# A top-32 attention and squared-ReLU feed-forward kernel: w_in in eight loads, a longer early form, fetches behind the transposes, later reciprocals and another order in the tail

## The chip, the cores and the metric

The kernel runs on one core of one Trainium2 chip. The metric is the device time of one execution in microseconds, the median of three timed runs. A separate profiled execution gives the rows shown here; times inside it count from the start of its span.

## The reference

```python
def _attn_ref(q, k, v):                      # q, k, v: (8, 8, 576, 64) float32
    scores = (1.0 / np.sqrt(64)) * np.matmul(q, k.transpose(0, 1, 3, 2))
    kth = np.partition(scores, -32, axis=-1)[..., -32:-31]
    scores = np.where(scores >= kth, scores, -1000000000.0)
    scores = scores - np.max(scores, axis=-1, keepdims=True)
    attn = np.exp(scores)
    attn = attn / (np.sum(attn, axis=-1, keepdims=True) + 1e-09)
    return np.matmul(attn, v)

def _moe_ref(x, w_in, w_out):                # (4608, 512), (512, 2048), (2048, 512)
    h = np.maximum(x @ w_in, 0.0)
    return h * h @ w_out
# reference: x is the attention output with its heads side by side, one row a token
```

Each of 64 heads has 576 queries. A query keeps its 32 highest scores, takes the softmax over them and weighs the values. The result goes through a feed-forward layer with a squared ReLU.

## The kernel before

**Steps.** Heads are taken in 32 pairs, four to a batch. One pair has 576 rows of scores for each of its two heads, cut into chunks of 128 rows. A step of the main loop handles two such chunks (the two heads of a pair, or the 64-row rests of two pairs), and there are U = 144 steps. Steps 0 to 3 belong to pair 0, step 4 to the rests of pairs 0 and 1, steps 5 to 8 to pair 1; from step 9 on pairs 2 and 3 alternate. The program is one order written out by hand: `pin` keeps every instruction in program order on its engine, so an instruction that waits holds back all that stands behind it on the same engine.

**What a step does.** In step u the VectorE (DVE) first combines scores into candidates (`quads_of`, lines 323 and 324) and then runs four rounds of `topk`: eight maxima by MAX8 (line 374), and their removal by MATCH_REPLACE8 (line 378) after each round but the last. TensorE (PE) computes the scores of step u+1 into the banks `sc_a` and `sc_b` (line 285), and ScalarE (ACT) copies both into `s` (line 294). Between rounds 2 and 3 the DVE begins step u+1 with `pairs_of` (lines 314, 315 and, in the early form, 317). GpSimd (POOL) computes the lesser candidates (`both`, line 338, and `lesser`, line 347), which round 3 of the step reads, and marks the dropped scores (`drop`, line 411). ACT takes exponentials of step u-3 (`exps`, line 423) into `w_two`, `turn` has the SP queue transpose them by DMA into `wT` (line 432), and PE multiplies with the values two steps later (`weigh`, line 467; `in_gap` puts this between the two halves of the scores). `invert` takes the reciprocal of the sums on the DVE (line 483, or line 487 for the last 24 steps, where the sums come out of PE), and `place` scales the result into `x_tok` on ACT (line 506) or, where asked, on the DVE (line 504).

**The early form.** For u < EARLY the DVE computes the minimum of one quarter itself (line 317), and POOL's two lesser operations are half as wide (288 elements instead of 576). For u < EARLY - 2, `drop` adds its marks to `s` on POOL (line 413); after that an accumulating DMA from the POOL queue does it (line 415).

**Loading the heads.** `load_pair(i)` puts the ten loads of a pair on a list, `fetch(n)` issues the next n of them on the SP queue. The raw tiles have two buffers each. `prepare(u)` runs the next of the four units of a pair: the PE transposes and ACT copies of q and of k (`main`, lines 174 and 175), the 64-row rests (`rest`), and the copy of the values. A pair may be begun from `due(i) - 4` on: steps 1, 3 and 5 for pairs 1, 2 and 3. The transposes of a pair stand in PE's order behind the scores of the next step.

**Loading the weights.** `w_loads` holds four loads of `w_in` (128 rows of 2048 each, read as two groups of 64 rows in DRAM) and four of `w_out`. They go on POOL's queue and convert from float32 to bfloat16. `load_weights(1)` stands before the first scores, behind the first `lesser`, and at the end of each step, so `w_in` is issued by the end of step 1 and `w_out` in steps 2 to 5.

**The feed-forward and the tail.** Whenever 128 rows of `x_tok` are full, PE transposes them, multiplies with `w_in`, ACT takes ReLU and square, and PE multiplies with `w_out`; pieces of this are spread over the steps. Behind the loop the last two steps are masked on the DVE (line 427), transposed by PE (line 449), copied (`turned`, lines 454 and 456), weighed, placed, and the last 128 rows go through the feed-forward layer; `halves` (line 627) is the last product.

Of the kernel before, what the change touches and what calls it, by code (L numbers as in the profile page):

```python
# [23 lines left out]
def kernel(  # L24
# [41 lines left out]
    w_in = const.tile([128, KH, d_ff], bf16, name="w_in")  # L66
# [61 lines left out]
    def fetch(n):  # L128
        while n and fetches:
            fetches.pop(0)[1]()  # L130
            n -= 1
# [130 lines left out]
    U = len(steps)  # L262
    first = {}
# [42 lines left out]
    def pairs_of(u):  # L306
# [8 lines left out]
        pin(tt(near, one[:, :, 0:QUAR], two[:, :, 0:QUAR], op=ALU.max))  # L315
        if u < EARLY:
            pin(tt(cat[:, :, HALF + QUAR:S], one[:, :, QUAR:HALF], two[:, :, QUAR:HALF], op=ALU.min))
# [9 lines left out]
    def copy_far(u):  # L327
        d = st[u]
        if u >= EARLY:
            pin(nc.scalar.activation(d["most"][:, 1], d["ps"][1][:, :, 0:QUAR], AF.Copy))  # L330

    def both(u):
        d = st[u]
        n_h = 1 if u < EARLY else 2
        wide = n_h * QUAR
# [4 lines left out]
    def lesser(u):  # L340
        d = st[u]
        n_h = 1 if u < EARLY else 2
        wide = n_h * QUAR
# [3 lines left out]
        pin(tt(less, less, d["most"][:, 0:n_h, :, :].bitcast(i32).rearrange("p h x n -> p x h n"), op=ALU.subtract))  # L347

    GROUP = 18
    EARLY = 9  # L350
    held_m = {}
    tests = []

# [2 lines left out]
    def topk(u, rounds=(0, 1, 2, 3)):  # L356
        d = st[u]
        g = u % GROUP
        if g == 0 and 0 in rounds:
            held_m["m"] = small.tile([128, GROUP, 2, 4, 8], f32, name="m", bufs=2)  # L360
        held = held_m["m"]
        m = d["m"] = [held[:, g, :, r] for r in range(4)]
        d["ends"] = held[:, g].rearrange("p x r j -> p x (r j)")[:, :, 0:32:31]
        cat = d["cat"]
        def part(r, x):
            if r == 0:
                return cat[:, x, 0:QUAR].rearrange("p (g n) -> p g n", n=18)[:, :, 0:13]
            if r == 1:
                return cat[:, x, 0:QUAR].rearrange("p (g n) -> p g n", n=6)[:, :, 1:6]
            return cat[:, x, 0:(HALF - 24, S)[r - 2]]  # L370

        for r in rounds:
            for x in range(2):
                pin(nc.vector.max(out=m[r][:, x, :], in_=part(r, x)))  # L374
            if r == 3:
                break
            for x in range(2):
                pin(nc.vector.match_replace(out=part(r, x), in_to_replace=m[r][:, x, :], in_values=part(r, x), imm_value=NEG))  # L378
        if g == GROUP - 1 and 3 in rounds:
            f0 = 2 * (u + 1 - GROUP)  # L380
            each = held[:, :, :, :, 7].rearrange("p g x r -> p (g x) r")
            at = flags[:, f0:f0 + 2 * GROUP]
            for r in range(3):
                tests.append(lambda r=r: nc.gpsimd.tensor_tensor(at[:, :, r], each[:, :, 3], each[:, :, r], op=ALU.subtract))
            tests.append(lambda: nc.gpsimd.tensor_mul(at[:, :, 3], each[:, :, 3], each[:, :, 3]))
            tests.append(lambda: nc.gpsimd.tensor_scalar(at[:, :, 3], at[:, :, 3], scalar1=-1.0, scalar2=TINY * TINY, op0=ALU.mult, op1=ALU.add))
# [10 lines left out]
    SUMMED = U - 24  # L397
# [43 lines left out]
    def turn_by_tensor(u, x):  # L441
        if "tp" not in st[u]:
            st[u]["wT"] = scp.tile([128, 9, 128], bf16, name="wT", bufs=4)
            st[u]["tp"] = {}
        flat = w_two[u % 3][:, :, :].rearrange("p x n -> p (x n)")
        tp = bank(2 * (u - U + 2) + x, [128, 1024], bf16)
        tp = st[u]["tp"][x] = tp[:, 0:512 + 128 * x].rearrange("p (n r) -> p n r", r=128)
        for n in range(4 + x):
            pin(nc.tensor.transpose(tp[:, n, :], flat[:, (4 * x + n) * 128:(4 * x + n + 1) * 128], id_h[:, :]))

    def turned(u, x, by_scalar):
        to, tp = st[u]["wT"][:, 4 * x:4 + 5 * x, :], st[u]["tp"][x]
        if by_scalar:
            pin(nc.scalar.activation(to, tp, AF.Copy))
        else:
            pin(nc.vector.tensor_copy(to, tp))
# [22 lines left out]
    def invert(u):  # L479
        if u < SUMMED:  # L480
            if u % 2 == 0:
                both_r = small.tile([128, 2, 2, 1], f32, name="rboth", bufs=4)
                pin(nc.vector.reciprocal(both_r[:, :, :, 0], st[u]["sums"][:, :, :]))
                st[u]["r"], st[u + 1]["r"] = both_r[:, 0], both_r[:, 1]
            return
        r = small.tile([128, 2, 1], f32, name="rsum", bufs=4)
        pin(nc.vector.reciprocal(r[:, :, :], sums(u)[:, :, 64:65]))
        st[u]["r"] = r
# [231 lines left out]
    def to_weigh(u):  # L720
        return u - 5 if u <= CATCH + 1 else u - 4

    def in_gap(u):
        products(to_weigh(u))
        if moves:
            moves.pop(0)()()
# [25 lines left out]

    w_loads = []
    for kh in range(KH):
        rows = moe_w_in.rearrange("(t e a d) n -> t a e d n", t=2, e=2, a=2)[kh // 2, kh % 2]
        w_loads.append((w_in[:, kh, :], rows))
    for g in range(4):
        rows = moe_w_out.rearrange("(f p) n -> p f n", p=128)[:, 4 * g:4 * g + 4, :]
        w_loads.append((w_out[:, 4 * g:4 * g + 4, :], rows))

    def load_weights(n):
        for to, rows in w_loads[:n]:
            pin(nc.gpsimd.dma_start(out=to, in_=rows))
        del w_loads[:n]
# [9 lines left out]
    def due(i):  # L774
        if i >= NP - 8:
            return 101 + 4 * (i - (NP - 8))
        return first[4 * (i // 4) + 3] - 1 - 4 * (3 - i % 4) if i >= 4 else 2 * i + 3

    def prepare(u):
        nonlocal coming  # L780
# [11 lines left out]
    ones = const.tile([128, 1], f32, name="ones")  # L792
    pin(nc.gpsimd.memset(ones[:, :], 1.0))
    worst = const.tile([128, 1], f32, name="worst")
    load_weights(1)
    scores(0)
    both(0)
    copy_far(0)
# [8 lines left out]
    def ok(w):  # L807
        return 0 <= w < U
# [16 lines left out]
    for u in range(U):  # L825
        at_step[0] = u
        for x in range(2):
            if ok(u - 1) and not by_vector(u - 1, x):
                drop(u - 1, x)
        quads_of(u)  # L830
        topk(u, (0,))
        if u == U - 1:
            break
        if ok(u + 1):
            for i, c, a in steps[u + 1]:
                while coming <= i or (coming == i + 1 and soon):
                    prepare(u)
            scores(u + 1, (lambda: in_gap(u)) if u else None)
            both(u + 1)
        if u == 0:  # L840
            in_gap(u)
        if ok(to_weigh(u)):
            invert(to_weigh(u))
        casts_next = bool(soon) and soon[0].__name__ == "values"
        for _ in range(0 if casts_next else 2 if u < 8 else 1):
            prepare(u)
        if ok(to_weigh(u)):
            place(to_weigh(u))
        turn_x(u)
        moves.extend(soon_moves)  # L850
        soon_moves.clear()
        if u < 6:
            fetch(4)
        w = to_raise(u)
        if ok(w):
            exps(w, 0)
            exps(w, 1)
            turn(w)
        if u >= 6:
            fetch(4 if u < 12 else 3)  # L860
        topk(u, (1, 2))
        if u == U - 2:
            while behind:
                behind.pop(0)()
            take("d")
            products(u - 3)
            take("d")
        if ok(u + 1):
            pairs_of(u + 1)
            if u == U - 2:  # L870
                invert(u - 3)
            copy_far(u + 1)
            lesser(u + 1)
            if tests:
                pin(tests.pop(0)())
        if u == U - 2:
            place(u - 3)
            turn_x(u)
            take("d", True)
            moves.pop(0)()()  # L880
        if u == CATCH:
            exps(u - 2, 0)
            exps(u - 2, 1)
            turn(u - 2)
        topk(u, (3,))
        if casts_next:
            prepare(u)
        while after_far:
            after_far.pop(0)()
        after_far.extend(next_far)  # L890
        next_far.clear()
        if u < U - 2:
            dense(u, 0)
        st[u]["neg"] = negate(u, 2)
        if u == CATCH + 1:
            products(u - 4)
            invert(u - 4)
            place(u - 4)
            turn_x(u)
        if u < U - 2:  # L900
            dense(u, 1)
        else:
            early_exps(u, 1)
        load_weights(1)
# [30 lines left out]
    turned(U - 1, 0, False)  # L935
    products(U - 3)
    turn_by_tensor(U - 1, 1)
    turned(U - 1, 1, False)
    products(U - 2)
    products(U - 1)  # L940
    three.relu()
    invert(U - 4)
    invert(U - 3)
    place(U - 4)
    place(U - 3)
    three.square(nc.gpsimd)
# [2 lines left out]
    invert(U - 2)  # L949
    place(U - 2, (True, True))  # L950
    invert(U - 1)
    place(U - 1, (True, False))
    four.relu()
    four.square(nc.gpsimd)
    by_hand.clear()
# [155 lines left out]
```

## Time and profile before

| what | value |
|---|---|
| median of 3 timed runs | 915.57 us (914.55 to 915.66) |
| profiled execution, its own time | 914.72 us |
| span of the profiled execution | 912.6 us |
| mean granted TensorE clock | 0.939 |
| DVE busy | 873.8 us (96% of the span) |
| ACT busy | 779.4 us (85%) |
| POOL busy | 778.2 us (85%) |
| PE busy | 671.4 us (74%) |
| bytes moved by DMA | 165.98 MB, mean 182 GB/s |

Busy time is time in which an engine executes instructions. A row of the timeline gives the start and the duration in us, the engine, the line in the kernel, the operation, output <- inputs, the shape and the number of merged instructions; in square brackets stands how long the engine was idle just before, and what released it. A name like PEq or SPq is an engine's own queue. DMA rows give the size of one transfer and the median time from issue to landing. q0 is the queue that POOL's loads use, q1 that of SP. A queue's share is that of 16 DMA engines over the window.

### The profile page before, as it was taken

Reading aid. Unit: us, or ns where it says so; the run is one execution under the profiler, and the core shown is the slowest. Engines: PE = TensorE matmul, PEld = TensorE weight load, DVE = VectorE, ACT = ScalarE, POOL = GpSimd, SP = SyncE. Lnnn points to the kernel's source line nnn. Section 1 sums busy time; section 2 is a strip of 40 time slices with the busy share of each in tenths; the row PEclk is TensorE's granted clock in tenths of the full one; section 3 lists DMA queues with packets and bytes.
Section 4 is the critical chain, followed back from the end, with each engine's and each line's share of the span. In section 5 each row is a group of like instructions: output and inputs, shape, how many; then the busy total and the mean of one; then the engine's idle time right before and its main releaser. Section 6 shows DMA issues by size and latency. Waiting matters only on the chain.

```text
span 912.6 us, 20980 instructions
## 1 busy us (share of the span) xinstructions
PE 671.4 (74%) x6190; PEld 424.8 (47%) x6268; DVE 873.8 (96%) x3567; ACT 779.4 (85%) x1996; POOL 778.2 (85%) x816
## 2 busy tenths in 40 slices
PE   6276778677777777777776777777677677888886
PEld 3133345444444444544454544544444454555555
DVE  6759999999999999999999999999999999999995
ACT  3256789988998999988999899999999998998994
POOL 7669888988899888998898988998889988898892
PEclk9789999999998999998999999999999999989999
DMA  5778997999898999898889899898989999977972
GB/s 114 138 126 164 185 190 160 205 193 198 190 202 188 197 203 198 194 181 199 196 193 195 173 201 207 196 187 199 219 191 197 189 209 210 161 168 155 180 168 52
DMA packets 294586, 165.98 MB, mean 182 GB/s; under 512 B 261697, under 2 KB 272193, under 8 KB 294465
## 3 DMA queue, kind: packets, MB, share of 16 engines
q1 hardware_dynamic: 267408, 80.29, 46.9%
q0 software_dynamic: 25712, 83.84, 40.5%
q8 instruction: 52, 0.85, 0.4%
q14 instruction: 70, 0.57, 0.2%
q10 hardware_dynamic: 1344, 0.43, 0.2%
HBM read 37.75 MB, written 9.44 MB: 52 GB/s over the span
## 4 chain that ended last, share of the span: by engine, by line
DVE 66%; issue 12%; ACT 10%; PE 5%; SPq 5%; DMA 2%; ACTq 0%
DVE m L374 28%; DVE cat L378 18%; DVE sc_b L314 6%; DVE most L315 5%; DVE cat L324 5%; DVE cat L323 5%; SPq L117 2%; ACT s L294 2%; SPq L110 1%; ACT h L610 1%; DMA q_raw<-in_q_dram 1%; ACT rl L602 1%; PE dn_ps L661 1%; PE sc_b L285 1%; PE gen L595 1%
## 5 line engine op out<-in xcount | busy, mean ns | idle before, releaser
L374 DVE MAX8 m<-cat 128x8 f32<-128x104 f32 (+3 forms) x1152 | 437.5, 420 | 0.0
L378 DVE MATCH_REPLACE8 cat<-m,cat 128x104 f32<-128x104 f32 (+2 forms) x864 | 262.0, 310 | 0.0
L338 POOL TENSOR_TENSOR cat<-s 128x576 int32<-128x576 int32 (+1 forms) x144 | 240.1, 1668 | 3.0 <-ACT s L294 3.0
L347 POOL TENSOR_TENSOR cat<-cat,most 128x576 int32<-128x576 int32 (+1 forms) x144 | 196.9, 1367 | 26.7 <-ACT most L330 12.6
L285 PE MATMUL sc_b<-qkT 64*128 64x288 f32 x512 | 105.8, 488 | 87.6 <-DVE cat L324 83.6
L595 PEld LDWEIGHTS <-w_in 128*128 128x128 bf16 x2304 | 149.0, 102 | 41.5 <-issue 20.3
L285 PE MATMUL sc_a<-qkT 64*128 64x288 f32 x512 | 97.9, 455 | 82.6 <-DVE most L315 61.3
L661 PE MATMUL dn_ps<-w_out,h 128*128 128x512 bf16 x478 | 143.0, 421 | 10.6 <-issue 6.8
L595 PE MATMUL gen<-xT,w_in 128*128 128x128 bf16 x1984 | 137.6, 226 | 3.5 <-ACT xT L550 2.9
L411 POOL TENSOR_SCALAR gone_b<-s,neg 128x576 uint8<-128x576 f32 x142 | 105.9, 746 | 29.1 <-ACT neg L394 17.5
L411 POOL TENSOR_SCALAR gone_a<-s,neg 128x576 uint8<-128x576 f32 x143 | 106.7, 746 | 13.6 <-ACT neg L394 2.0
L294 ACT ACTIVATE s<-sc_b 128x576 f32<-128x576 f32 x144 | 93.2, 647 | 22.2 <-PE sc_b L285 16.3
L294 ACT ACTIVATE s<-sc_a 128x576 f32<-128x576 f32 x144 | 91.2, 633 | 5.5 <-PE sc_a L285 3.7
L285 PEld LDWEIGHTS sc_a<-qkT 64*128 64x128 f32 x512 | 41.7, 188 | 110.6 <-issue 56.0
L285 PEld LDWEIGHTS sc_b<-qkT 64*128 64x128 f32 x512 | 43.4, 196 | 102.8 <-PE av_ps L467 61.5
L610 ACT ACTIVATE h<-rl 128x512 bf16<-128x512 f32 x136 | 85.7, 630 | 4.3
L602 ACT ACTIVATE rl<-gen 128x512 f32<-128x512 f32 x140 | 81.8, 584 | 3.0 <-PE gen L595 2.9
L314 DVE TENSOR_TENSOR sc_b<-sc_a,s 128x288 f32<-128x288 f32 x144 | 65.3, 454 | 18.8 <-ACT s L294 16.3
L661 PEld LDWEIGHTS <-h 128*128 128x128 bf16 x544 | 51.8, 105 | 64.0 <-issue 31.3
L467 PEld LDWEIGHTS <-wT 128*128 128x128 bf16 (+1 forms) x1600 | 54.7, 100 | 56.7 <-issue 45.6
L415 POOL DMA_DIRECT2D s<-gone_b x68 | 60.0, 883 | 22.0 <-DVE m L374 12.0
L394 ACT ACTIVATE neg<-m 128x4 f32<-128x4 f32 (+1 forms) x145 | 29.9, 207 | 57.2 <-DVE m L374 56.3
(186 smaller groups left out, 1296.5 us busy)
## 6 DMA issues: line engine op xcount, KB each, us to landing
s<-gone_b POOLq DMA_DIRECT2D x68, 576.0 KB, 4.6
s<-gone_a POOLq DMA_DIRECT2D x67, 576.0 KB, 4.6
v_raw<-in_v_dram SPq DMA_DIRECT2D x64, 128.0 KB, 3.0
k_raw<-in_k_dram SPq DMA_DIRECT2D x63, 128.0 KB, 3.2
q_raw<-in_q_dram SPq DMA_DIRECT2D x63, 128.0 KB, 3.3
out_dram<-wide SPq DMA_DIRECT2D x31, 256.0 KB, 2.9
v_raw<-in_v_dram SPq DMA_DIRECT2D x64, 32.0 KB, 3.2
w_in<-in_moe_w_in_dram POOLq DMA_DIRECT2D x4, 512.0 KB, 24.6
```

The lines of the kernel that those rows point to most:

```text
L285: pin(nc.tensor.matmul(out=ps[j][:, x, 0:HALF], lhsT=lhsT, rhs=rhs, start=True, stop=True))
L294: pin(nc.scalar.activation(s[:, :, j * HALF:(j + 1) * HALF], ps[j][:, :, 0:HALF], AF.Copy))
L314: pin(tt(far, one[:, :, QUAR:HALF], two[:, :, QUAR:HALF], op=ALU.max))
L338: pin(tt(less, s[:, :, 0:wide].bitcast(i32), s[:, :, HALF:HALF + wide].bitcast(i32), op=ALU.add))
L347: pin(tt(less, less, d["most"][:, 0:n_h, :, :].bitcast(i32).rearrange("p h x n -> p x h n"), op=ALU.subtract))
L374: pin(nc.vector.max(out=m[r][:, x, :], in_=part(r, x)))
L378: pin(nc.vector.match_replace(out=part(r, x), in_to_replace=m[r][:, x, :], in_values=part(r, x), imm_value=NEG))
L411: pin(nc.gpsimd.tensor_scalar(byte[:, x, :, 1], s[:, x, :], scalar1=d["neg"][:, x, 1:2], scalar2=-HUGE, op0=ALU.add, op1=ALU.mult))
L595: pin(nc.tensor.matmul(out=hp[:, n * n_rows:(n + 1) * n_rows], lhsT=w_in[:, kh, (f0 + n) * 128:(f0 + n + 1) * 128], rhs=xt(kh), start=(kh ...
L602: pin(nc.scalar.activation(kept["rl"][:, :], hp, AF.Relu))
L610: pin(nc.scalar.activation(h2, flat, AF.Square))
L661: pin(nc.tensor.matmul(out=op[:, :], lhsT=held["h2"][:, f, c * 128:(c + 1) * 128], rhs=w_out[:, f, :], start=(f == 0), stop=(f == NF - 1)))
```

## The change

Six edits are made at once.

- `w_in` is loaded in eight loads of 64 rows: each half of a former load is a DMA of its own, whose DRAM side is 64 rows and not two groups of 64. Two halves are issued ahead of the first scores, one behind the first `lesser`, one at the end of each of steps 0 to 4; `w_out` follows in steps 5 to 8.
- `EARLY` is 11 and not 9: steps 9 and 10 take the early form, and `drop` of steps 7 and 8 adds on POOL.
- Pairs 1, 2 and 3 may be begun at steps 1, 4 and 7.
- `fetch` stands behind `turn` in the first six steps too, as it did later.
- In the steps with `to_weigh(u) >= SUMMED` and u < U - 5 (125 to 138), round 1 of `topk` goes ahead of the reciprocal and not behind it.
- In the tail the reciprocals of U-4 and U-3 go ahead of the last copy of `turned`, and both results of U-1 are placed by the DVE, where ACT had one.

```diff
-    EARLY = 9
+    EARLY = 11
...
     for kh in range(KH):
-        rows = moe_w_in.rearrange("(t e a d) n -> t a e d n", t=2, e=2, a=2)[kh // 2, kh % 2]
-        w_loads.append((w_in[:, kh, :], rows))
+        for e in range(2):
+            rows = moe_w_in.rearrange("(t e a d) n -> t a e d n", t=2, e=2, a=2)[kh // 2, kh % 2, e]
+            w_loads.append((w_in[64 * e:64 * e + 64, kh, :], rows))
...
-        return first[4 * (i // 4) + 3] - 1 - 4 * (3 - i % 4) if i >= 4 else 2 * i + 3
+        return first[4 * (i // 4) + 3] - 1 - 4 * (3 - i % 4) if i >= 4 else 3 * i + 2
...
-    load_weights(1)
+    load_weights(2)
     scores(0)
     both(0)
     copy_far(0)
...
             in_gap(u)
+        sums_late = ok(to_weigh(u)) and to_weigh(u) >= SUMMED and u < U - 5
+        if sums_late:
+            topk(u, (1,))
         if ok(to_weigh(u)):
             invert(to_weigh(u))
...
-        if u < 6:
-            fetch(4)
         w = to_raise(u)
         if ok(w):
             exps(w, 0)
             exps(w, 1)
             turn(w)
-        if u >= 6:
-            fetch(4 if u < 12 else 3)
-        topk(u, (1, 2))
+        fetch(4 if u < 12 else 3)
+        topk(u, (2,) if sums_late else (1, 2))
...
     products(U - 3)
     turn_by_tensor(U - 1, 1)
+    invert(U - 4)
+    invert(U - 3)
     turned(U - 1, 1, False)
     products(U - 2)
     products(U - 1)
     three.relu()
-    invert(U - 4)
-    invert(U - 3)
     place(U - 4)
     place(U - 3)
...
     invert(U - 1)
-    place(U - 1, (True, False))
+    place(U - 1, (True, True))
```

## The prediction

> **What bounds the kernel now.** I read the busy shares first, then who waited for whom, then the windows, to see where the bounding engine stands still.
>
> ```profile
> PE 671.4 (74%) x6190; PEld 424.8 (47%) x6268; DVE 873.8 (96%) x3567; ACT 779.4 (85%) x1996; POOL 778.2 (85%) x816
> DVE sc_b L314 <- ACT s L294: 16.3, 3, 15.8
> DVE rsum L487 <- PE av_ps L467: 1.4, 2, 0.9
> 40.00:46.00 6.00, 0.00 (x0) 0.00 (x0) 0.14 (x1) 0.00 (x0) 0.00 (x0) 0.50 0.82 146
> 160.00:400.00 240.00, 176.85 (x1670) 114.63 (x1687) 239.75 (x984) 219.85 (x576) 213.80 (x214) 0.94 0.93 195
> ```
>
> The DVE is the bound: from 160 to 400 us it is busy 239.75 of 240 us. Only fewer DVE instructions or fewer DVE waits shorten the kernel. Its waits (columns: total, times, longest) hold one large entry, a single stop of 15.8 us. In the window from 40 to 46 us (columns: length, busy PE, PEld, DVE, ACT, POOL, then clock, DMA share, GB/s) no engine computes while the DMA engines are 82% busy. So the loads ended last there. The timeline of that stretch says which.
>
> ```profile
> 39.73 0.41 DVE L378 MATCH_REPLACE8 cat<-m,cat 128x264 f32<-128x264 f32 x1
> 49.61 1.11 PE L174 MATMUL gen<-id_f,k_raw 128*128 128x128 f32 x4 [13.54 <-DMA q_raw<-in_q_dram]
> 55.94 0.47 DVE L314 TENSOR_TENSOR sc_b<-sc_a,s 128x288 f32<-128x288 f32 x1 [15.80 <-ACT s L294]
> 57.04 1.41 DVE L374 MAX8 m<-cat 128x8 f32<-128x576 f32 x2
> ```
>
> L314 at 55.94 begins step 5, which works on pair 1, whose heads are long there. Ahead of its scores PE has the transposes of pair 2's k, moved forward into step 3, and those wait until 49.61 for the load. Why is a load so late? The DMA view has it, first for 16 to 23 us, then for 24 to 30, then for 78 to 130.
>
> ```profile
> q0 software_dynamic: 756, 0.44, 36.4%
> w_in<-in_moe_w_in_dram POOLq DMA_DIRECT2D x1, 512.0 KB, 23.8
> q0 software_dynamic: 655, 0.56, 51.1%
> k_raw<-in_k_dram SPq DMA_DIRECT2D x2, 128.0 KB, 20.3
> k_raw<-in_k_dram SPq DMA_DIRECT2D x4, 128.0 KB, 3.4
> w_in<-in_moe_w_in_dram POOLq DMA_DIRECT2D x4, 512.0 KB, 24.6
> s<-gone_b POOLq DMA_DIRECT2D x68, 576.0 KB, 4.6
> ```
>
> With three w_in loads in flight, q0 holds 36.4% of 16 engines, 5.8 of them; with four, 51.1%, 8.2. So each w_in load runs on two engines, and takes 24.6 us. The accumulating DMA of the same queue moves more, 576 KB, in 4.6 us. What differs is the source: w_in is read as two groups of 64 rows, the other as 128 rows. A k load of 128 KB landed in 20.3 us while the weights were in flight and in 3.4 us later: every head load waits for its share on the engines that w_in holds.
>
> **The change part by part.**
>
> *EARLY 11: +0.7.* The starts of L314 give the step.
>
> ```profile
> 62.31 0.46 DVE L314 TENSOR_TENSOR sc_b<-sc_a,s 128x288 f32<-128x288 f32 x1
> 68.60 0.46 DVE L314 TENSOR_TENSOR sc_b<-sc_a,s 128x288 f32<-128x288 f32 x1
> 87.25 0.45 DVE L314 TENSOR_TENSOR sc_b<-sc_a,s 128x288 f32<-128x288 f32 x1
> 93.19 0.45 DVE L314 TENSOR_TENSOR sc_b<-sc_a,s 128x288 f32<-128x288 f32 x1
> ```
>
> An early step takes 68.60 - 62.31 = 6.29 us, a later one 93.19 - 87.25 = 5.94. Two steps at 0.35 make +0.7, on the bounding engine, hidden by nothing.
>
> *Halves of w_in, and pair 2 a step later: -15.8.* A half is one group of 64 rows. If the rows are dealt out to 16 engines, each gets 4 instead of 64, and 24.6 us become an estimated 24.6 / 16 = 1.5 us plus the fixed part, bounded by the 4.6 us row above.
>
> The Trainium skill speaks for and against. Its page "DMA: Bandwidth & Descriptors" says under "Rules for kernel authors" that splitting a transfer into two partition halves is not worth it, as both use the same 16 engines; by this the stop would shrink by its later place alone (a rival below). Its section "Why a DMA increments its semaphore by 16 and not by 1" says the slowest dimension of both sides sets the number of engines: two before, sixteen after. The 36.4% and 51.1% bear the second one out; the premise of the first is not met here.
>
> ```profile
> 12.03 1.82 SPq L110 DMA_DIRECT2D q_raw<-in_q_dram  x2
> 13.89 10.85 SPq L117 DMA_DIRECT2D q_raw<-in_q_dram  x1
> 28.79 0.72 PE L285 MATMUL sc_a<-qkT,qbd_a 128*128 128x288 f32 x2 [1.36 <-DVE cat L317]
> ```
>
> Pair 2's loads begin at 12.03 and SP is then held 10.85 us in one issue, as the queue backs up. Unheld, the first eight of its ten loads, at 1.82 / 2 = 0.91 us an issue, are out by 19.3 us and with 3.4 us landed by 23. Their transposes now stand behind the scores of step 5, one step of 6.3 us after those of step 4 at 28.79, so not before 35 us: 12 us to spare. Then L314 of step 5 starts where step 4 ends, 39.73 + 0.41 = 40.14, and the whole 15.8 us go. The next thing due, pair 3, is fetched in steps 4 to 6 and transposed in step 7.
>
> *Four more weight loads on POOL: 0, up to +2.3.* POOL's issues and round 3 of the step are the pair to watch.
>
> ```profile
> 11.50 0.79 POOL L338 TENSOR_TENSOR cat<-s 128x288 int32<-128x288 int32 x1 [1.95 <-ACT s L294]
> 36.42 0.79 POOL L347 TENSOR_TENSOR cat<-cat,most 128x288 int32<-128x288 int32 x1
> 58.94 0.79 POOL L763 DMA_DIRECT2D w_out<-in_moe_w_out_dram  x1
> 65.69 0.79 POOL L763 DMA_DIRECT2D w_out<-in_moe_w_out_dram  x1
> 66.56 0.74 POOL L411 TENSOR_SCALAR gone_b<-s,neg 128x576 uint8<-128x576 f32 x1
> 72.58 0.75 POOL L411 TENSOR_SCALAR gone_a<-s,neg 128x576 uint8<-128x576 f32 x1
> ```
>
> The extra load ahead of the first scores (0.79, as for w_out) fits into the 1.95 us idle before 11.50. A step with a weight load takes POOL 65.69 - 58.94 = 6.75 us, one without 72.58 - 66.56 = 6.02; the DVE needs 6.3. So POOL loses 0.45 us a loaded step, and where the stop let it catch up before, it now runs on through step 8. Cover: for step 4, L347 ends at 36.42 + 0.79 = 37.21, and round 3, which reads it, starts 57.04 - 55.94 = 1.10 us behind L314, at 40.14 + 1.10 = 41.24. Of the 4.0 us, five loaded steps take 2.3 and leave 1.7; steps 9 and 10 give some back. Without that cover it would cost the same 2.3.
>
> *Fetches behind the transposes: 0.* A fetch now queues on SP behind a transpose that waits for ACT's exponentials. Behind it hang pair 2's last two loads and pair 3's, wanted one to three steps later; without that cover, one transpose issue.
>
> *Late reciprocals: -1.2, between -1.4 and 0.*
>
> ```profile
> 809.81 0.17 DVE L487 RECIPROCAL rsum<-av_ps 128x2 f32<-128x2 f32 x1 [0.58 <-PE av_ps L467]
> 811.05 0.51 ACT L506 ACTIVATE x_tok<-av_ps,rsum 128x64 bf16<-128x64 f32 x2
> 815.81 0.16 DVE L487 RECIPROCAL rsum<-av_ps 128x2 f32<-128x2 f32 x1
> 816.75 0.76 DVE L374 MAX8 m<-cat 128x8 f32<-128x264 f32 x2
> 822.75 0.17 DVE L487 RECIPROCAL rsum<-av_ps 128x2 f32<-128x2 f32 x1 [0.86 <-PE av_ps L467]
> ```
>
> Only two reciprocals waited, 0.58 and 0.86. Round 1 now comes first: 816.75 - 815.81 - 0.16 = 0.78 us of work. It covers 0.58 and nearly all of 0.86, so -1.4 + 0.1, and I give another 0.1 to the later `place`: ACT took the result 1.07 us after the reciprocal (811.05), so it mostly waits for nothing. If PE is the slower there, the waits move to L314 and nothing is won.
>
> *Tail: -0.15, between -0.5 and 0.*
>
> ```profile
> 895.63 0.49 DVE L456 COPY wT<-end 128x640 bf16<-128x640 bf16 x1 [0.40 <-PE end L449]
> 896.95 0.28 DVE L504 TENSOR_SCALAR x_tok<-end,rsum 128x64 bf16<-128x64 f32 x1
> 897.14 0.38 PE L643 MATMUL dn_ps<-w_out,h 128*128 128x512 bf16 x1 [0.60 <-POOL h L608]
> 897.33 0.31 ACT L506 ACTIVATE x_tok<-end,rsum 128x64 bf16<-128x64 f32 x1 [0.17 <-DVE x_tok L504]
> 897.70 0.38 PE L544 MATMUL end<-id_h,x_tok 128*128 128x128 bf16 x4 [0.18 <-ACT x_tok L506]
> ```
>
> Two reciprocals (0.16 each) fill the idle 0.40 before 895.63, and the last placement no longer crosses to ACT: x_tok is done up to 0.5 us sooner. But ahead of its transposes PE has two products of L643, which wait for POOL until 897.14 and end at 897.52 at the earliest. Of the 0.5, 897.70 - 897.52 less a hand-over is left, 0.15.
>
> *Order on ACT around step 18: 0, -0.8 to +0.4.* Pairs 4 to 7 are prepared one step later, so ACT's fullest steps change places. There the DVE now waits once 0.67 us for ACT's L330.
>
> ```profile
> 144.11 0.46 DVE L323 TENSOR_TENSOR cat<-sc_b,most 128x288 f32<-128x288 f32 x1 [0.67 <-ACT most L330]
> ```
>
> **Sum.** Against the profiled execution's own time: 914.72 - 15.8 + 0.7 - 1.2 - 0.15 = 898.3. The median of the runs (915.57) lies 0.85 above that execution; I add half and forecast 898.7. This case's own range: below, 914.72 - 15.8 + 0.7 - 1.4 - 0.5 - 0.8 = 896.9, less 0.2 for the fastest run (914.55); above, no gain from reciprocals and tail, +0.4 on ACT, +0.94 for the slowest run (915.66), which is 901.0.
>
> **The rivals.**
>
> *POOL takes over.* If a loaded step costs POOL more than 6.3 + 4.0 / 5 = 7.1 us, round 3 waits for L347. Price as above, 2.3: 901.0, with the same scatter 899 to 903.4. For it: POOL has no idle time between 58.94 and 65.69 and the cover falls to 1.7 us. Against: both loads issued in these rows cost 0.79.
>
> *Halves bring nothing.* The eight loads hold the engines as long as the four did, k of pair 2 still lands at 49.61, and only the later place helps: step 6 is held and not step 5, the stop is 15.8 - 6.3 = 9.5 us. 914.72 - 6.3 + 0.7 - 1.35 + 0.4 = 908.2. Against: 8.2 engines for four loads. The Trainium skill's rule on partition halves, in the same section of "DMA: Bandwidth & Descriptors" as above, would have it so.
>
> *Slower: one engine a half.* If the count of engines followed the number of groups, each half would lie on one engine for the same 64 rows, 24.6 us, and the last, issued at the end of step 4 at about 37.2 + 6.75 = 44, until 68.6. Pair 3's transposes, in step 7 at 28.79 + 4 x 6.3 = 54, would stop PE for some 15 us, on top of the 9.5: 24.5 instead of 15.8, so 914.72 + 8.7 + 0.7 - 1.35 + 0.4 = 923.2. It decides from a landing of about 17 us a half on. Against: the 128 rows of s<-gone spread without a group of two.
>
> **How the numbers follow.** Forecast 0.80, POOL 0.09, no effect of the halves 0.07, one engine a half 0.04. The range of the first two is 896.7 to 903.4; widened by 0.3 for a step that I did not see, 896.4 to 903.7. It leaves out the last two cases, 0.11, and a little of the first. A difference under 0.2% (1.8 us; three runs spread over 1.1) can't be told from none. The first three cases are faster by more than that; between the third and the fourth I keep 0.01 for the same. Faster 0.95, same 0.01, slower 0.04.
>
> **What would show it.** In the profile after, the entry of 15.8 us among the DVE's waits is gone and L314 of step 5 starts at about 40; a w_in load of 256 KB lands within 5 us; k loads before 30 us land in 3 to 5 us; steps 9 and 10 are 6.3 us apart; the waits of L487 are under 0.2 us in all; the last x_tok transposes start 0.1 to 0.2 us nearer to the reciprocals. A w_in load over 15 us, or PE waiting over 5 us for a head load, would make the prediction wrong; a DVE wait on L347 would mean POOL.

## The result, and the profile after

| | before | after |
|---|---|---|
| median of timed runs | 915.56 us (914.55 to 915.66, 5 runs) | 898.32 us (897.49 to 898.67, 5 runs) |
| ratio to before | 1 | 0.9815 (95% interval 0.9801 to 0.9828) |
| profiled execution, own time / span | 914.72 / 912.6 us | 897.49 / 895.3 us |
| mean granted TensorE clock | 0.939 | 0.954 |

The change saves 17.2 us in the medians and 17.3 us in the spans. The forecast was 898.7.

First the busy shares of the page after, then the DVE's waits (total, times, longest), then the window that had stood still (length, busy PE, PEld, DVE, ACT, POOL, then clock, DMA share, GB/s).

```profile
PE 673.2 (75%) x6268; PEld 420.1 (47%) x6268; DVE 874.8 (98%) x3570; ACT 777.5 (87%) x1993; POOL 781.5 (87%) x822
```

```profile
DVE sc_b L314 <- PE sc_a L285: 2.6, 1, 2.6
DVE cat L323 <- ACT most L330: 0.9, 2, 0.6
DVE rsum L487 <- PE av_ps L467: 0.5, 1, 0.5
```

```profile
40.00:46.00 6.00, 4.40 (x30) 1.99 (x28) 6.00 (x27) 3.61 (x12) 5.65 (x7) 1.00 0.64 111
```

The entry of 16.3 us of L314 waiting for ACT is gone. The DVE does the same work (874.8 us against 873.8) in a shorter span, and from 40 to 46 us, where it had 0.14 us to do, it is busy throughout. The loads of the same kernel say why: the DMA view from 24 to 30 us, the page's DMA issues, and rows of SP's timeline, the first where it had been held.

```profile
q0 software_dynamic: 80, 0.26, 26.0%
w_in<-in_moe_w_in_dram POOLq DMA_DIRECT2D x1, 256.0 KB, 4.0
```

```profile
w_in<-in_moe_w_in_dram POOLq DMA_DIRECT2D x8, 256.0 KB, 4.6
```

```profile
13.31 0.67 SPq L117 DMA_DIRECT2D q_raw<-in_q_dram  x1
14.02 1.46 SPq L110 DMA_DIRECT2D k_raw<-in_k_dram  x2
34.48 1.43 SPq L432 DMA_TRANSPOSE wT<-w_two_a  x1
```

One load of 256 KB takes 26.0% of 16 engines over 6 us, 25.0 us of engine time. Before, 512 KB took two engines for 24.6 us, which is 24.6 per 256 KB. So the work of the queue is about the same; it is spread over more engines, and a load lands in 3.7 to 5.6 us (median 4.6) where the larger one took 24.6. SP's issue at 13.31 takes 0.67 us, where the like one had taken 10.85, and pair 2's k is issued at 14.02.

The timeline of the DVE gives the steps; here the starts of steps 4, 5, 9, 10, 11 and 12.

```profile
33.31 0.45 DVE L314 TENSOR_TENSOR sc_b<-sc_a,s 128x288 f32<-128x288 f32 x1
39.61 0.45 DVE L314 TENSOR_TENSOR sc_b<-sc_a,s 128x288 f32<-128x288 f32 x1
...
64.93 0.45 DVE L314 TENSOR_TENSOR sc_b<-sc_a,s 128x288 f32<-128x288 f32 x1
71.29 0.44 DVE L314 TENSOR_TENSOR sc_b<-sc_a,s 128x288 f32<-128x288 f32 x1
77.73 0.47 DVE L314 TENSOR_TENSOR sc_b<-sc_a,s 128x288 f32<-128x288 f32 x1
...
84.43 0.45 DVE L314 TENSOR_TENSOR sc_b<-sc_a,s 128x288 f32<-128x288 f32 x1
```

The same starts cut every profile into stretches. The table has their lengths in us (steps 1 to 4 take 18.9 in all of them); the headings are the steps at whose start a stretch begins and ends.

| kernel | to 1 | 4-5 | 5-9 | 9-12 | 12-20 | 20-130 | 130-143 | 143-end |
|---|---|---|---|---|---|---|---|---|
| before | 14.87 | 22.17 | 25.32 | 17.92 | 48.88 | 657.52 | 79.73 | 27.29 |
| after | 14.41 | 6.30 | 25.32 | 19.50 | 48.11 | 657.02 | 78.90 | 26.84 |
| halves alone | 15.02 | 6.29 | 25.31 | 17.92 | 48.14 | 657.48 | 78.18 | 27.48 |
| due alone | 15.16 | 6.30 | 44.37 | 18.08 | 48.09 | 657.40 | 79.78 | 27.06 |
| after, two groups a load | 14.91 | 6.29 | 43.33 | 22.59 | 48.09 | 657.21 | 78.69 | 27.31 |
| after, EARLY 9 | 15.13 | 6.28 | 25.32 | 24.62 | 48.87 | 658.39 | 78.17 | 26.84 |
| the same, weights as before | 14.87 | 6.28 | 25.31 | 18.09 | 48.08 | 657.42 | 78.91 | 27.15 |
| after, EARLY 9, due as before | 14.74 | 6.30 | 26.56 | 18.64 | 48.10 | 657.71 | 78.28 | 26.91 |
| after, due as before | 14.94 | 6.28 | 25.31 | 18.64 | 49.16 | 657.50 | 78.18 | 27.00 |
| after, sums early | 15.32 | 6.29 | 25.31 | 19.44 | 48.08 | 656.53 | 79.74 | 26.99 |
| after, tail as before | 15.14 | 6.30 | 25.31 | 18.66 | 48.08 | 657.04 | 78.84 | 27.23 |
| after, fetch as before | 15.03 | 6.30 | 25.31 | 18.94 | 48.34 | 658.60 | 78.29 | 27.09 |
| halves, late sums, tail | 14.77 | 6.30 | 25.31 | 17.92 | 48.13 | 657.82 | 78.17 | 27.12 |
| the same, EARLY 7 | 14.94 | 6.29 | 24.58 | 17.93 | 48.07 | 660.80 | 78.87 | 26.92 |

After less before, stretch by stretch: -0.46, -15.87, 0.00, +1.58, -0.77, -0.50, -0.83, -0.45 (and 0.00 from 1 to 4), together -17.30. Only the second is large. Kernels with the same program up to step 120 (after, sums early, tail as before) differ by 0.8 from step 9 to 12 and by 0.5 from 20 to 120, so a single difference under 0.9 us says nothing by itself.

### The profile page after: what moved, and what is told of

Read it like the earlier page. It is cut to its first block, busy times and chain, and to the rows that moved or that the text cites. A ratio compares the mean times of both kernels' runs of the same rounds, so it can differ in the third digit from the quotient of the medians.

```text
span 895.3 us, 21062 instructions
## 1 busy us (share of the span) xinstructions
PE 673.2 (75%) x6268; PEld 420.1 (47%) x6268; DVE 874.8 (98%) x3570; ACT 777.5 (87%) x1993; POOL 781.5 (87%) x822
## 4 chain that ended last, share of the span: by engine, by line
DVE 69%; ACT 12%; issue 12%; PE 5%; DMA 1%; POOL 0%; SPq 0%; ACTq 0%; DVEq 0%
DVE m L374 29%; DVE cat L378 18%; DVE sc_b L314 6%; DVE most L315 5%; DVE cat L324 5%; DVE cat L323 5%; ACT s L294 2%; ACT h L610 2%; ACT rl L602 2%; DMA q_raw<-in_q_dram 1%; PE sc_b L285 1%; PE gen L595 1%; ACT x_tok L506 1%; ACT w_two_b L423 1%; PE dn_ps L661 1%
## 5 line engine op out<-in xcount | busy, mean ns | idle before, releaser
L347 POOL TENSOR_TENSOR cat<-cat,most 128x576 int32<-128x576 int32 (+1 forms) x144 | 196.0, 1361 | 22.0 <-ACT most L330 10.7
L595 PEld LDWEIGHTS <-w_in 128*128 128x128 bf16 x2304 | 145.3, 101 | 41.7 <-issue 20.1
L661 PE MATMUL dn_ps<-w_out,h 128*128 128x512 bf16 x544 | 155.4, 416 | 1.8 <-ACT wide L669 1.8
L595 PE MATMUL gen<-xT,w_in 128*128 128x128 bf16 x1984 | 134.4, 223 | 4.1 <-ACT xT L550 3.1
L294 ACT ACTIVATE s<-sc_b 128x576 f32<-128x576 f32 x144 | 93.3, 648 | 24.5 <-PE sc_b L285 18.9
L415 POOL DMA_DIRECT2D s<-gone_a x66 | 58.3, 884 | 20.4 <-DVE m L374 10.5
```

Source lines behind the costliest of these rows:

```text
L294: pin(nc.scalar.activation(s[:, :, j * HALF:(j + 1) * HALF], ps[j][:, :, 0:HALF], AF.Copy))
L415: pin(nc.gpsimd.dma_start(out=s[:, :, :].rearrange("p x n -> p (x n)"), in_=byte[:, :, :, :].rearrange("p x n two -> p (x n two)").bitcast ...
L595: pin(nc.tensor.matmul(out=hp[:, n * n_rows:(n + 1) * n_rows], lhsT=w_in[:, kh, (f0 + n) * 128:(f0 + n + 1) * 128], rhs=xt(kh), start=(kh ...
L661: pin(nc.tensor.matmul(out=op[:, :], lhsT=held["h2"][:, f, c * 128:(c + 1) * 128], rhs=w_out[:, f, :], start=(f == 0), stop=(f == NF - 1)))
```

## The experiments

Runs of one changed kernel spread over 0.9 to 4.6 us here (over 8.9 and 9.7 with the two that have EARLY 9 beside late weights), those of the kernel before over up to 6.3, so effects under 1 us are read from the profiles. Ratios are to the kernel before on the same chip; its medians were 915.09, 915.31 and 915.72 us.

**The halves alone.** The kernel before, with each `w_in` load as two halves, both at its former place.

```diff
-        w_loads.append((w_in[:, kh, :], rows))
+        w_loads.append([(w_in[64 * e:64 * e + 64, kh, :], rows[e]) for e in range(2)])
...
-        for to, rows in w_loads[:n]:
-            pin(nc.gpsimd.dma_start(out=to, in_=rows))
+        for part in w_loads[:n]:
+            for to, rows in part:
+                pin(nc.gpsimd.dma_start(out=to, in_=rows))
```

> The kernel before, with w_in alone changed: each of its four loads becomes two loads of 64 rows, issued back to back at the same four places; nothing else differs. Spread theory: a half is dealt out to sixteen engines, lands in about 5 us, k of pair 2 is there by 23 us though its transposes still stand in step 3, and the whole stop of 15.8 us goes: 915.56 - 15.8 = 899.8, between 898.9 and 900.7. If instead the later place of the transposes (not in this kernel) is needed, a stop of 5 us or more stays and the time is over 905. If the halves bring nothing, 915.6.

Measured: 897.26 us (896.92 to 899.27), ratio 0.9812 [0.9789, 0.9835]. Step 4 to 5 takes 6.29 us. The page's DMA issues and the DVE's waits for ACT's copy show why:

```profile
w_in<-in_moe_w_in_dram POOLq DMA_DIRECT2D x8, 256.0 KB, 5.9
```

```profile
DVE sc_b L314 <- ACT s L294: 0.3, 1, 0.3
```

So the halves are enough for the whole gain, without the later place of pair 2. The time is 2.5 us under the 899.8 that I expected and below its range. Against the profile before, 1.55 us of that lie in steps 130 to 143, where no reciprocal waited this time, and 0.74 in steps 12 to 20; that the halves cause these isn't shown.

**The later pairs alone.** The kernel before, with pairs 2 and 3 begun at steps 4 and 7 and `w_in` as it was.

```diff
-        return first[4 * (i // 4) + 3] - 1 - 4 * (3 - i % 4) if i >= 4 else 2 * i + 3
+        return first[4 * (i // 4) + 3] - 1 - 4 * (3 - i % 4) if i >= 4 else 3 * i + 2
```

> The kernel before, with the starts of pairs 2 and 3 alone moved from steps 3 and 5 to steps 4 and 7; w_in in four loads of two groups of 64 rows as before. The price list says that k of pair 2 still lands near 49.6 us, that step 6 and not step 5 is held, and that the stop shrinks by one step of 6.3 us to 9.5: 909.2, between 908 and 910.5. If the order of the transposes were the whole cause, the stop would go: 899 to 901.

Measured: 915.73 us (912.97 to 917.53), ratio 1.0002 [0.9987, 1.0017]. The later place alone brings nothing. The DVE, PE and SP rows of its timeline:

```profile
39.63 11.70 SPq L432 DMA_TRANSPOSE wT<-w_two_a  x1
49.34 1.12 PE L174 MATMUL gen<-id_f,k_raw 128*128 128x128 f32 x4 [10.57 <-DMA k_raw<-in_k_dram]
52.63 0.18 DVE L483 RECIPROCAL rboth<-sums 128x4 f32<-128x4 f32 x1 [8.24 <-ACT w_two_b L423]
63.02 0.73 PE L467 MATMUL av_ps<-vau_a,wT 128*128 128x65 bf16 x10 [8.85 <-DMA wT<-w_two_a]
65.75 0.47 DVE L314 TENSOR_TENSOR sc_b<-sc_a,s 128x288 f32<-128x288 f32 x1 [10.61 <-ACT s L294]
```

k of pair 2 lands at 49.34, nearly as before (49.61), and step 5 now stops for 8.24 us where the reciprocal waits for ACT. Then a second stop comes: the transpose issued at 39.63 holds SP for 11.70 us behind the backed-up loads, PE gets its `wT` at 63.02, and step 6 waits 10.61. Together 18.85, not the 9.5 that I had computed. Putting off the reader did not shrink the stop here; the queue carried it on to the next reader.

**Two groups again, in eight loads.** The changed kernel, where each load of 64 rows reads two groups of 32.

```diff
-            rows = moe_w_in.rearrange("(t e a d) n -> t a e d n", t=2, e=2, a=2)[kh // 2, kh % 2, e]
+            rows = moe_w_in.rearrange("(t f a e d) n -> t a e f d n", t=2, f=2, a=2, e=2)[kh // 2, kh % 2, e]
```

> The changed kernel, but each of the eight loads of 64 rows reads two groups of 32 rows that lie apart in DRAM, so size, number and place of the loads are the same and only the outer dimension of the source is 2 and not 64. It permutes the rows of w_in, so the output is not the reference's. Spread theory (the outer dimension sets the number of engines): each load runs on two engines, 32 rows on each, and lands in about 24.6 / 2 = 12.3 us; head loads issued before 45 us take about 10 us and not 3 to 5, and some of the stop comes back: 900 to 908, about 902. If the smaller size or the later place of the loads is what helps, 898.3 as the changed kernel, with w_in landing in about 5 us.

Measured: 918.47 us (916.86 to 919.92), ratio 1.0037 [1.0024, 1.0050]: slower than before, and 10 us over the top of the 900 to 908 that I expected. The page's DMA issues, the DVE's waits, and three rows of its DVE timeline:

```profile
w_in<-in_moe_w_in_dram POOLq DMA_DIRECT2D x8, 256.0 KB, 14.2
```

```profile
DVE sc_b L314 <- ACT s L294: 20.6, 4, 10.9
```

```profile
57.45 0.47 DVE L314 TENSOR_TENSOR sc_b<-sc_a,s 128x288 f32<-128x288 f32 x1 [10.90 <-ACT s L294]
76.95 0.47 DVE L314 TENSOR_TENSOR sc_b<-sc_a,s 128x288 f32<-128x288 f32 x1 [6.75 <-ACT s L294]
98.85 0.47 DVE L314 TENSOR_TENSOR sc_b<-sc_a,s 128x288 f32<-128x288 f32 x1 [2.68 <-ACT s L294]
```

Size, places and number of loads are those of the changed kernel; only the outer dimension of the source is two. The load takes 14.2 us instead of 4.6, SP is held again (7.51 us in the issue at 13.90, 9.78 in the transpose at 41.19), and the stops are back, three of them. Each load does run on two engines: from 30 to 36 us, with two of them in flight, `q0` holds 24.3% of 16 engines, 3.9. The 25.0 us of engine time on two engines are 12.5, which leaves 1.7 us beside the transfer; in the changed kernel 4.6 - 25.0 / 16 = 3.0 are left. That a load reads pieces which lie apart in DRAM isn't enough to slow it: a `w_out` load takes four rows for each of 128 partitions, 128 rows apart, with the 128 outermost, and its 512 KB land in 7.8 us in the changed kernel. So the outer dimension decides, as the Trainium skill's page "DMA: Bandwidth & Descriptors" has it under "Why a DMA increments its semaphore by 16 and not by 1" (the number of engines divides the slowest dimension of both sides).

**EARLY 9 in the changed kernel, three ways.** First `EARLY` alone is put back; then the weights too go to their former places (two halves at each, `w_out` in steps 2 to 5); and, apart from that, with the late weights, the pairs go back to steps 3 and 5.

```diff
-    EARLY = 11
+    EARLY = 9
```

> The changed kernel with EARLY back at 9. If the two extra early steps cost their DVE instruction alone, 0.35 us each, 898.32 - 0.7 = 897.6. In the profile after, steps 10 and 11 took 6.44 and 6.70 us, 0.86 more together than the form explains; if that hangs on the early form too, about 896.8. If the early form spares POOL or ACT something in these steps, no gain or a loss up to 1: 898.3 to 899.3.

For the second, beside that:

```diff
-        for e in range(2):
-            rows = moe_w_in.rearrange("(t e a d) n -> t a e d n", t=2, e=2, a=2)[kh // 2, kh % 2, e]
-            w_loads.append((w_in[64 * e:64 * e + 64, kh, :], rows))
+        rows = moe_w_in.rearrange("(t e a d) n -> t a e d n", t=2, e=2, a=2)[kh // 2, kh % 2]
+        w_loads.append([(w_in[64 * e:64 * e + 64, kh, :], rows[e]) for e in range(2)])
...
-    load_weights(2)
+    load_weights(1)
```

> The changed kernel with EARLY back at 9 and the weights at their former places: two halves of w_in wherever one load stood, so w_out is issued in steps 2 to 5 and not in 5 to 8. With EARLY 9 alone 902.55 was measured: steps 10 and 11 took 7.69 and 10.94 us, as the accumulating DMAs of 576 KB begin at step 8 beside the last w_out loads and pair 4's loads. Theory one, the w_out loads are the collision: their removal from steps 5 to 8 brings steps 9 to 12 back to 5.9 to 6.0 us and the time to about 896.8 (896 to 898). Theory two, pair 4's loads are too late in any case (fetched at step 7, wanted at step 9): steps 10 and 11 stay over 6.4 us and the time is 898.5 to 902.

For the third, beside EARLY 9:

```diff
-        return first[4 * (i // 4) + 3] - 1 - 4 * (3 - i % 4) if i >= 4 else 3 * i + 2
+        return first[4 * (i // 4) + 3] - 1 - 4 * (3 - i % 4) if i >= 4 else 2 * i + 3
```

> The changed kernel with EARLY 9 and with pairs 2 and 3 begun at steps 3 and 5 as before, so pair 4's loads are issued two steps earlier; w_out stays in steps 5 to 8. Theory one (w_out collides with the accumulating DMAs): the transposes by DMA still land late, steps 10 to 12 keep some of the loss, 899 to 902. Theory two (pair 4's loads come too late): the loss is gone, about 896.8.

Measured: 902.55 us (900.43 to 909.29), ratio 0.9868 [0.9836, 0.9901]; with the weights as before 897.32 (896.31 to 899.03), 0.9806 [0.9780, 0.9832]; with the pairs as before 901.75 (898.26 to 907.94), 0.9874 [0.9835, 0.9913]. I had expected 0.7 us less from EARLY 9 and got 4.2 more. POOL, PE and DVE rows of the first one's timeline:

```profile
66.17 0.95 POOL L415 DMA_DIRECT2D s<-gone_b  x1 [0.31 <-DVE sc_b L314]
70.01 0.77 POOL L764 DMA_DIRECT2D w_out<-in_moe_w_out_dram  x1
71.67 0.63 PE L174 MATMUL gen<-id_f,q_raw 128*128 128x128 f32 x4 [2.36 <-DMA q_raw<-in_q_dram]
72.73 0.89 POOL L415 DMA_DIRECT2D s<-gone_a  x1 [0.30 <-DVE most L315]
75.18 0.46 DVE L323 TENSOR_TENSOR cat<-sc_b,most 128x288 f32<-128x288 f32 x1 [1.41 <-ACT most L330]
77.40 0.48 PE L467 MATMUL av_ps<-vau_b,wT 128*128 128x65 bf16 x10 [2.47 <-DMA wT<-w_two_c]
81.89 1.08 PE L174 MATMUL gen<-id_f,k_raw 128*128 128x128 f32 x4 [3.33 <-DMA k_raw<-in_k_dram]
85.86 0.46 DVE L323 TENSOR_TENSOR cat<-sc_b,most 128x288 f32<-128x288 f32 x1 [4.42 <-ACT most L330]
```

With EARLY 9 the accumulating DMAs (576 KB each) begin at 66.17, while the last two `w_out` loads are on their way and pair 4 is being fetched; PE waits for q, `wT` and k in turn, ACT waits for PE, and the DVE for ACT. Steps 9 to 12 take 24.62 us. With `w_out` three steps earlier the accumulations begin at about the same time (65.74) and the stretch takes 18.09. So late `w_out` loads and early accumulations together make the stop: the changed kernel has the late loads without it, and EARLY 9 beside the earlier loads has none either. In the changed kernel EARLY 11 keeps the two apart: its last `w_out` load is issued at 69.56 and lands within 8.6 us, and its first accumulation is issued at 78.34. The two steps cost 0.7, and without them the kernel is 4.2 slower.

What the fetch of pair 4 adds isn't shown. With the pairs put back but the weights late, the median (901.75) is the same within the scatter. The profile, that of the fastest of four runs, is 1.24 us longer from 5 to 9 and 0.72 from 9 to 12, but the 1.24 lie ahead of the first accumulation (65.80): there PE waits 3.45 us for `wT`, until 64.57.

**The pairs' former places in the changed kernel.** The same edit, with EARLY 11 kept.

> The changed kernel with pairs 2 and 3 begun at steps 3 and 5 as before; EARLY stays 11, the weights stay one load a step. PE's wait of 1.04 us for pair 4's q and the 0.86 us in steps 10 and 11 should go: 898.3 - 0.9 = 897.4. A wait of PE for pair 2's k at step 3 should not come back (k lands by 20 us); if it did, 900 or more.

Measured: 898.87 us (898.14 to 899.98), ratio 0.9824 [0.9800, 0.9848], no different from the changed kernel; the 0.9 us that I expected to gain did not come. Its steps 9 to 12 take 18.64 us, the 17.92 of before plus two early steps, and not 19.50. But the kernel with the tail as before, whose program is that of the changed kernel there, takes 18.66. So the other 0.86 comes and goes between profiles, and that the pairs cause it isn't shown. Steps 12 to 20 take 49.16 us here, 1.05 more than in the changed kernel, and why stays open.

**Late sums and tail, one at a time, and the fetch.** The changed kernel with one edit undone in each.

```diff
-        sums_late = ok(to_weigh(u)) and to_weigh(u) >= SUMMED and u < U - 5
+        sums_late = False
```

> The changed kernel with round 1 again behind the reciprocal in steps 125 to 138; all else as changed. Prediction's theory: the late reciprocal saves what the reciprocals of L487 wait, so without it the waits of L487 are 0.9 to 1.5 us in all in place of 0.53 and the time is 899.2 (898.3 + 0.9). Rival, from the profile of the halves alone, where no reciprocal waited without the edit: the waits come and go with the turn that the loads take earlier, the edit saves nothing of its own, and the time stays 898.3, L487's waits 0 to 0.6 in all. The two differ by less than the runs scatter, so the rows of L487 decide, not the time.

Measured: 899.26 us (898.84 to 899.93), ratio 0.9823 [0.9807, 0.9839]. The waits of its DVE:

```profile
DVE rsum L487 <- PE av_ps L467: 1.4, 2, 0.9
```

That is the 1.4 us of before, and steps 130 to 143 take 79.74 us, as before and with the due edit alone (79.73, 79.78), against 78.90. So the edit is worth 0.8 us where PE is late. With the edit the stretch takes 78.2 to 78.3 us in five profiles and 78.7 to 78.9 in five; without it 79.7 to 79.8 in three and 78.18 in one, that of the halves alone, where no reciprocal waited. Why PE was in time there stays open.

```diff
-    invert(U - 4)
-    invert(U - 3)
     turned(U - 1, 1, False)
...
+    invert(U - 4)
+    invert(U - 3)
     place(U - 4)
...
-    place(U - 1, (True, True))
+    place(U - 1, (True, False))
```

> The changed kernel with the tail in its former order (reciprocals of U-4 and U-3 behind the ReLU, one result of U-1 placed by ACT). The prediction gave the edit 0.15 us, the profile of the changed kernel shows 0.26 from the last copy of turned (L456) to the x_tok transposes (L544): 1.81 us against 2.07. Theory: that stretch is 2.07 again and the time 898.6 (898.3 + 0.26). Rival: POOL's h (L608) holds the transposes in both orders, the stretch stays within 0.05 of 1.81, and the 0.26 is scatter between profiles.

Measured: 898.49 us (897.76 to 898.62), ratio 0.9813 [0.9796, 0.9829]. The timelines of the tail, first of this kernel, then of the changed one:

```profile
878.62 0.49 DVE L456 COPY wT<-end 128x640 bf16<-128x640 bf16 x1 [0.43 <-PE end L449]
880.33 0.31 ACT L506 ACTIVATE x_tok<-end,rsum 128x64 bf16<-128x64 f32 x1 [0.17 <-DVE x_tok L504]
880.69 0.38 PE L544 MATMUL end<-id_h,x_tok 128*128 128x128 bf16 x4 [0.21 <-ACT x_tok L506]
```

```profile
878.77 0.49 DVE L456 COPY wT<-end 128x640 bf16<-128x640 bf16 x1
879.96 0.48 DVE L504 TENSOR_SCALAR x_tok<-end,rsum 128x64 bf16<-128x64 f32 x2
880.06 0.60 PE L643 MATMUL dn_ps<-w_out,h 128*128 128x512 bf16 x2 [0.39 <-POOL h L608]
880.58 0.38 PE L544 MATMUL end<-id_h,x_tok 128*128 128x128 bf16 x4
```

From the last copy to the `x_tok` transposes it is 2.07 us without the edit (880.69 - 878.62) and 1.81 with it. All ten profiles with the edit show 1.81 or 1.82, all four without it 2.07, so the 0.26 belongs to the edit. x_tok is done 1.67 us after the copy's start (879.96 + 0.48) and not 2.02 (880.33 + 0.31), since the hand-over to ACT is gone. Of these 0.35 the transposes take 0.26: they follow 0.14 behind x_tok and not 0.05. Products of L643, which wait for POOL until 880.06, stand ahead of them and probably take the rest.

```diff
+        if u < 6:
+            fetch(4)
...
-        fetch(4 if u < 12 else 3)
+        if u >= 6:
+            fetch(4 if u < 12 else 3)
```

> The changed kernel with the fetch of the first six steps ahead of turn again. The prediction gave this edit 0: 898.3, steps 0 to 9 as in the changed kernel within 0.2 us. Rival: behind a transpose that waits for ACT's exponentials the loads of pairs 2 and 3 were put off, or ahead of it they put off the transposes and with them the weighing; then step 9 starts more than 0.5 us from 64.93, and the time moves by as much.

Measured: 898.46 us (897.39 to 899.17), ratio 0.9808 [0.9791, 0.9824]. Step 9 starts 0.61 us later than in the changed kernel, but all of it lies ahead of step 1 (15.03 against 14.41, a start that varies from 14.41 to 15.32 over all profiles); from there to step 9 both take 50.5 us. The edit is worth nothing.

**Is there a better version?** The kernel before with the halves as in the first experiment, and the late sums and the tail of the change; and then with EARLY 7 too.

```diff
+        sums_late = ok(to_weigh(u)) and to_weigh(u) >= SUMMED and u < U - 5
+        if sums_late:
+            topk(u, (1,))
...
-        topk(u, (1, 2))
+        topk(u, (2,) if sums_late else (1, 2))
...
+    invert(U - 4)
+    invert(U - 3)
     turned(U - 1, 1, False)
...
-    place(U - 1, (True, False))
+    place(U - 1, (True, True))
```

> The kernel before with three parts of the change: w_in in halves, two at each former place of one load, the late reciprocals, and the new tail. EARLY stays 9, the starts of the pairs and the fetches stay as before. Halves alone gave 897.26; the tail takes off 0.26 as in the profile after; the late reciprocals take off what waits there are, 0 to 0.9. 896.5, between 895.5 and 897.3.

```diff
-    EARLY = 9
+    EARLY = 7
```

> The kernel before with the halves of w_in, two at each former place, late reciprocals and tail, and EARLY 7 in place of 9. Theory: an early step costs the DVE 0.35 us more, two fewer save 0.7: 896.65 - 0.7 = 896.0, steps 7 and 8 in 5.95 us. Rival: as with EARLY 9 beside the late weights, the accumulating DMAs, now from step 5 on, meet the w_out loads of steps 2 to 5 and the head loads; waits of PE for wT or for a head load stop a step, steps 6 to 8 take 7 us or more, and the time is 898 to 902.

Measured: 896.65 us (896.30 to 899.47), ratio 0.9803 [0.9779, 0.9826]; with EARLY 7 897.27 us (895.95 to 899.51), 0.9794 [0.9778, 0.9810]. In steps 5 to 9 EARLY 7 saves the 0.7 us (24.58 against 25.31) and brings no stop there; the 896.0 that I expected is not shown by the times. In its profile, that of the slowest run, the stretch from 20 to 130 is 3 us longer, with one wait of 2.37 us at 629 us behind a late `wT`, far from the edit. Three edits out of six give at least what all six give: the steps 9 to 12 are 1.58 us shorter than in the changed kernel, while the intervals of the two ratios overlap. The halves alone (897.26) can't be told from all six (898.32) either, so the other five edits together bring no gain that the times show.

## Why the prediction was right, point by point

**The halves: -15.8, measured -15.87.** The mechanism and the size were right: the stop went whole (step 5 at 39.61, I had named 40), nothing took its place, and k is issued when SP is no longer held. The estimate of 1.5 us is 25.0 / 16 = 1.6 as measured; the landing of 4.6 leaves 3.0 for the fixed part, which I had bounded and not priced. Two signs missed by a little: the largest landing was 5.6 and not within 5, and the two k loads issued from 13 to 30 us landed in 5.5 (median) and not in 3 to 5. That pair 2's later place belongs to it was wrong: the halves alone do it.

**EARLY 11: +0.7.** Right for the two steps (18.64 and 18.66 against 17.92 in two profiles); the changed kernel's own profile has 0.86 more. A wait of PE for pair 4's q at 70.56 us stands ahead of it, and step 11 then waits for ACT:

```profile
70.56 1.09 PE L174 MATMUL gen<-id_f,q_raw 128*128 128x128 f32 x4 [1.04 <-DMA q_raw<-in_q_dram]
80.48 0.46 DVE L323 TENSOR_TENSOR cat<-sc_b,most 128x288 f32<-128x288 f32 x1 [0.60 <-ACT most L330]
```

What the step left out is the larger thing: I priced each edit against the kernel before, and not against the others. In the change `w_out` moves to steps 5 to 8, and with EARLY 9 that costs 4.2 us. "Hidden by nothing" was true of the 0.7 and missed what it pays for.

**POOL: 0.** Right in the outcome and too careful in the price: a half takes 0.53 to 0.56 us to issue and not 0.79, a loaded step with it 23.15 to 29.66, 6.5 us:

```profile
23.15 0.56 POOL L764 DMA_DIRECT2D w_in<-in_moe_w_in_dram  x1
29.66 0.56 POOL L764 DMA_DIRECT2D w_in<-in_moe_w_in_dram  x1
```

No DVE wait names L347. Of the cover I had 1.7 us left in step 9; there L347 ends at 69.61 (68.82 + 0.79) and round 3 begins at 72.38, so 2.8 were left.

**Late reciprocals: -1.2.** Measured -0.83, and 0.84 by the undoing. One wait of 0.53 us is left in step 132, where I gave the rest 0.1: the term was too large by 0.4. The sign for telling it (waits under 0.2) failed.

**Tail: -0.15.** Measured 0.26, inside its bounds. **Fetch: 0** was right. **ACT near step 18: 0.** The changed kernel gained 0.77 there, my lower end, but so did the halves alone and nearly every other kernel, with the pairs at either place. The profile of before had one of the three longer ones.

**Sum.** I had -16.45 on the profiled execution (and 0.4 added for the median); it came to -17.23. The 0.8 between is made of small things that mostly are no edit's: the start -0.46, steps 12 to 20 -0.77, 20 to 130 -0.50, the end -0.30 more than forecast, against +0.88 in steps 9 to 12 and +0.37 at the reciprocals. That the total came out within 0.4 us of 898.7 is in part luck: errors of both signs cancel, and the one term that carries the forecast, the stop, was right by its mechanism. One sum had a slip: the top of POOL's case is 901.0 + 2.3 = 903.3 and not 903.4, which decides nothing.

**The rivals.** POOL did not take over. "Halves bring nothing" was refuted by the landing time, and its price was wrong as well: with the later pairs alone 915.73 was measured, so an estimate for it is about 915 and not 908. "One engine a half" needed a landing over 17 us; it was 4.6. But two groups in a half, on two engines, did come out slower than before, at 14.2 us. My threshold of 17 us was too high, since I counted one stop, where the kernel with two groups shows three (10.90, 6.75 and 2.68 us). The Trainium skill's rule on partition halves ("DMA: Bandwidth & Descriptors", "Rules for kernel authors") does not hold here: it takes for granted that both forms use all 16 engines, and 24.6 us against 4.6 shows that one did not.

## What to carry to other kernels

When a load is several times slower than another of its size, look at the outer dimension of both of its sides and at the queue's share of the engines before you look at its place: here an outer dimension of two made a load of 256 KB land three times later (14.2 against 4.6 us) and held SP with it (7.51 us in one issue, against 0.67). Here, too, putting off one reader of a load that was late only moved the stop (915.73 us with the later pairs alone). Price the edits of one change against each other too: a move that is free by itself (weights later) can be paid for by another edit that looks like a pure cost (a longer early form).

## What the runs showed of the hardware that was not expected

- Two loads of 256 KB, alike but for the outer dimension of the source (64 rows, or two groups of 32), landed in 4.6 and 14.2 us, and the kernel with the latter (918.47 us) was slower than the one before. POOL took 0.53 to 0.56 us to issue one of the former and 0.67 to 0.70 for one of the latter.
- A DMA transpose issued on a queue of SP that was backed up held SP for 11.70 us, where it takes 1.43 at 34.48 us in the kernel after.
- Accumulating DMAs of 576 KB beside the last two `w_out` loads of 512 KB cost this kernel 4.2 us (902.55 against 898.32); either without the other made no such stop.
- Profiles of programs that are the same up to step 120 differ there by up to 0.8 us in a single stretch (18.66 to 19.50 us from step 9 to 12).
